# A two-layer convolution and a joint network on one core: weight sums in fp16, shift copies dropped, 378 direct outputs for 426

## The chip, the cores and the metric

The kernel runs on one core of a Trainium2 chip. The metric is device time in microseconds of one execution, given as the median of several runs. A separate execution was taken with the hardware profiler; its page and its trace are what the readings below come from. Engines are named as the profile names them: PE is TensorE's matmuls and PEld its weight loads, DVE is VectorE, ACT is ScalarE, POOL is GpSimd, SP is SyncE, which issues nearly all DMAs.

## What is computed

x is 2 x 4000 x 512 in bf16, w1 and w2 are five 512 x 512 taps each, and the three last weights are 512 x 512.

```python
xp = jnp.pad(x, ((0,0),(pad,pad),(0,0)))          # pad = 2
for i in range(5):
    h = h + einsum("btc,cd->btd", xp[:, i:i+T, :], w1[i])
h = gelu(h)[:, ::2, :]                             # 2 x 2000 x 512
# the same once more with w2:                        f = gelu(...)[:, ::2, :], 2 x 1000 x 512
fe = einsum("btd,de->bte", f, w_f)
ge = einsum("bud,de->bue", g, w_g)                 # g: 2 x 8 x 512
j = tanh(fe[:, :, None, :] + ge[:, None, :, :])    # 2 x 1000 x 8 x 512
return einsum("btud,dv->btuv", j, w_o)
```

## The kernel before

**Two ways to compute the first convolution.** A convolution with stride 2 and five taps needs 5 x 16 matmuls (four blocks of 128 input channels, four of output channels) per column of outputs. The kernel does the first `ND` = 426 outputs of the first sequence that way, tap by tap (`direct`, in the order `TAPS` = 0, 4, 2, 1, 3). All others are computed in triples (`Triple`, `Unit`): three neighbouring outputs come out of 9 products instead of 15, on sums and differences of x and on sums of the weight taps that are made once. A product of a triple is 16 matmuls over n columns for 3n outputs. The first sequence has a small set of `NF` = 190 triples (tile `xa`) and one of 336 (`xp1`); the second sequence has two of 334 (`xp2`, `xp0`). The second convolution is two more sets of 334 (`hT0`, `hT1`) on the first one's output. The tiles `row0` and `row1` hold the x differences of even samples, the planes of `xa` and `xp` are overwritten with those of odd samples.

**Getting x in.** For the direct part x is loaded in rows (`xr`): 512 rows with four samples a partition, then 384 rows with three a partition. `turn` transposes the first block on TensorE (16 transposes against `ident`), `turn3` the second with 12 matmuls against permutation matrices (`perm`) that POOL builds; ACT and DVE evict both to `eo`, split into even and odd samples. For the triples x comes through DMA transposes, six phases a set (samples 6q to 6q + 5).

**Weight sums.** `w1part` and `w2part` make the summed taps for one block of 128 output channels each: t = w0 + w4, v = t - w2, u = w0 + 4 w4 + 2 w2, t + w2, w1 - w3, w1 + w3, 2 w1. t, u and v are float32 (`ssum`, `wv`, `wu`, `ws`). u is made by two scalar_tensor_tensor on DVE (`stt`, line 655); ACT scales u and v by 1/3 into bf16, and makes 2 w1.

**x differences** (`step`, sums on line 494, copies on line 499). Three planes r = 2z - z' are made by an ACT copy with scale 2 and a DVE subtraction. Two more ACT copies, "next" and "prev", shift a plane by one column, so that the sums "ti" and "s0" read columns that start where their output starts.

**A unit** is one block of 128 output channels of one set. It runs its nine products into a PSUM bank of its own in five pieces; between these ACT copies the bank aside (tile `sd`) and DVE combines it (line 655, `acc<-acc,sd`), and ACT applies gelu. Units follow each other with one to two in flight.

**The joint part**, from about 130 us on, forms tanh on ACT and multiplies with w_o by a seven-product scheme on 2 x 2 blocks (`Seven`) whose operand sums go to POOL or DVE.

**Order.** Each engine's instructions are placed by a planner: every operation is recorded with what it reads and writes, and `schedule` lays them out with estimated costs; `once` is one pass, `learn` shifts priorities, and up to `PASSES` = 1200 passes are tried. Operations recorded with `flex` may go to ACT or DVE (or POOL or DVE); the planner picks. `emit` then adds the semaphore waits. All matmuls have one line in the profile, 507, all DVE sums line 494, all ACT operations line 499.

Of the kernel before, what the change touches and what calls it, by code (L numbers as in the profile page):

```python
# [12 lines left out]
P = 128  # L13
CELL = 4

# [53 lines left out]
class Plan:  # L69
# [4 lines left out]
    PASSES = 1200  # L74
# [85 lines left out]
    def schedule(self, pred):  # L160


        ops, HOP, n = self.ops, self.HOP, len(self.ops)
        succ = [[] for _ in ops]
        for i, p in enumerate(pred):
            for j in p:
                succ[j].append(i)
        span = [o.cost + (4.0 if o.dma else 0.0) for o in ops]
        late, nextpe = [0.0] * n, 0.0
        for i in range(n - 1, -1, -1):  # L170
            t = min([late[s] - (HOP if pred[s][i] else ops[i].cost - span[i]) for s in succ[i]], default=0.0)
            if ops[i].eng == "pe":
                t = min(t, nextpe)
            late[i] = t - span[i]
            if ops[i].eng == "pe":
                nextpe = late[i]
        hold = [0.0] * n
        best, tried = self.once(pred, succ, late, hold), 0
        for _ in range(self.PASSES):
            new = list(late), list(hold)  # L180
            if not self.learn(pred, best, *new, tried):
                break
            got = self.once(pred, succ, *new)
            if got[0] < best[0] + 1e-9:
                tried = tried + 1 if got[0] > best[0] - 1e-9 else 0
                best, (late, hold) = got, new
            else:
                tried += 1
        self.end, order, self.start, _, _, where = best
        for i, e in where.items():  # L190
            o = ops[i]
            o.eng, (o.fn, o.cost), o.alt = e, o.alt[e], None
        return order

    def learn(self, pred, got, late, hold, tried):


        _, order, start, end, ready, _ = got
        place = {i: (e, p) for e, o in order.items() for p, i in enumerate(o)}
        gaps, t = [], 0.0  # L200
        for i in order["pe"]:
            if start[i] - t > 0.05 and start[i] > 6.0:
                gaps.append(i)
            t = end[i]
        if not gaps:
            return False
        kind, which = divmod(tried, len(gaps) + 1)
        if kind >= 6:
            rng = np.random.default_rng([13, tried])
            t = start[gaps[int(rng.integers(len(gaps)))]]  # L210
            for e in ("act", "dve"):
                for j in order[e]:
                    if t - 10.0 < start[j] < t and rng.random() < 0.15:
                        late[j] += float(rng.normal())
            return True
        step, wait = ((0.1, True), (0.5, False), (0.0, True), (2.0, True), (0.3, False), (1.0, True))[kind % 6]
        first = list(late)
        for i in gaps if which == len(gaps) else gaps[which:which + 1]:
            j = i
            for _ in range(30):  # L220
                done = [(end[q] + (self.HOP if w else 0.0), q) for q, w in pred[j].items()]
                if not done:
                    break
                q = max(done)[1]
                if self.ops[q].dma:
                    break
                e, p = place[q]
                if e in ("act", "dve") and p and start[q] > ready[q] + 0.03:
                    b = order[e][p - 1]
                    if wait and start[b] < ready[q] - 0.02 and first[b] > first[q]:  # L230
                        hold[b] = max(hold[b], ready[q] - 0.01)
                    late[q] -= step
                j = q
        return True

    def once(self, pred, succ, late, hold):


        ops, HOP, n = self.ops, self.HOP, len(self.ops)
        left = [len(p) for p in pred]  # L240
        ready = list(hold)
        free = {e: 0.0 for e in ("pe", "act", "dve", "pool", "sp")}
        cand = {e: [] for e in free}
        engines = [o.alt or (o.eng,) for o in ops]
        for i in range(n):
            if not left[i]:
                for e in engines[i]:
                    cand[e].append(i)
        order, where = {e: [] for e in free}, {}
        wire, lock, owner, start, done = 0.0, 0.0, None, [0.0] * n, [0.0] * n  # L250
        for _ in range(n):
            best = None
            for e, c in cand.items():
                if c:
                    t = max(free[e], min(ready[i] for i in c))
                    if best is None or t < best[0]:
                        best = (t, e)
            t, e = best
            now = [i for i in cand[e] if ready[i] <= t + 0.02]
            i = min(now) if e in ("pe", "sp", "pool") else min(now, key=lambda i: (late[i], i))  # L260
            for f in engines[i]:
                cand[f].remove(i)
            order[e].append(i)
            o = ops[i]
            cost = o.cost
            if o.alt:
                where[i], cost = e, o.alt[e][1]
            start[i] = t
            free[e] = t + cost
            if o.port:  # L270
                if owner != e and lock > t - 0.2 and e == "dve":
                    free[e] = max(t, lock) + cost + 0.2
                elif owner != e and lock > t:
                    free[e] = lock + cost
                lock, owner = free[e], e
            done[i] = end = free[e]
            if o.dma:
                wire = max(wire, t + 1.8) + o.wire
                end = max(wire, t + 2.0) + o.slack
            for s in succ[i]:  # L280
                ready[s] = max(ready[s], end + HOP if pred[s][i] else free[e])
                left[s] -= 1
                if not left[s]:
                    for f in engines[s]:
                        cand[f].append(s)
        return max(free.values()), order, start, done, ready, where
# [82 lines left out]
def bass_standalone__seq2seq_rnn_t_joint__speech_kernel(  # L369
# [26 lines left out]
    ND, NF = 426, 190  # L396
    NL = 2 * NT3 - ND // 3 - NF
    assert ND % 6 == 0 and NF % 2 == 0 and NL % 2 == 0
    EW = 16 + 4 * P
# [10 lines left out]
    with ExitStack() as es:  # L410
# [28 lines left out]
        ssum = [at(f"ssum{i}", [NK, P], FP32) for i in range(2)]  # L439
        geT = at("geT", [NK * BU], FP32)  # L440
        gT = at("gT", [NK, BU], BF16)
        zero = at("zero", [NT], BF16)
        ident, perm = at("ident", [P], BF16), at("perm", [3 * P // 2], BF16)
# [4 lines left out]
        assert eo.end <= w2_sb.end and ND < 4 * P  # L448
        xa = Buf(nc, "xa", [7, NK, 224], BF16, xs[0].end - xs[0].bytes)
# [70 lines left out]
        for i in range(3):  # L520
            pm = perm[i * P // 2:(i + 1) * P // 2]
            pl.op("pool", lambda e, pm=pm, i=i: e.affine_select(
                out=pm.ap, in_=zero[0:P // 2].ap, compare_op=ALU.not_equal, fill=1.0, base=-(i % 2),
                pattern=[[-2, P // 2]], channel_multiplier=1), (zero[0:P // 2],), (pm,))
# [7 lines left out]
        NR = (4, 3)  # L532
# [76 lines left out]

        def turn(pp, cost):  # L610
# [21 lines left out]
        def turn3(cost):  # L632
            n, h, lo = NR[1], P // 2, 16 + 2 * P
            for k in range(NK):
                c0 = (4 + k) * NT
                at_k = ps.cols(c0, 2 * n * h)

                def fn(e, k=k, c0=c0):
                    for r in range(n):
                        if r % 2:  # L640
                            o, pm = ps.h[:, c0 + 2 * h:c0 + 4 * h], perm.h[:, h:3 * h]
                        else:
                            o = ps.h[:, c0:c0 + NT].rearrange("p (s c) -> p s c", c=h)[:, r // 2:r // 2 + 5:4, :]
                            pm = perm.h[:, 0:2 * h].rearrange("p (s c) -> p s c", s=2)
                        ins = e.matmul(o, lhsT=xr[1].h[:, r, k, :], rhs=pm, start=r == 0, stop=r == n - 1,  # L645
                                       skip_group_check=True)
                    return ins
                pl.op("pe", fn, (xr[1][0:n], perm[:]), (at_k,), cost / NK)
# [10 lines left out]
        def w2part(m, part):  # L659
            sl = slice(m * P, (m + 1) * P)  # L660
            w = lambda i: w2_sb[i, :, sl]
            t, v, u = ssum[0][:], ssum[1][:], ws[0][:]
            if part == "s":
                tt("dve", t, w(0), w(4), add)
                tt("dve", v, t, w(2), sub)
# [694 lines left out]
```

## Time and profile before

| | |
|---|---|
| Time, median of 3 runs | 251.72 us (251.39 to 251.92) |
| Profiled execution, span from first to last instruction | 249.7 us |
| Median time beyond that span | 2.0 us |
| PE busy, share of the span | 245.6 us, 98% |
| DVE busy | 209.2 us, 84% |
| ACT busy | 210.4 us, 84% |
| POOL busy | 99.3 us, 40% |
| Granted TensorE clock | 1.00 |

The profiled execution has no other time than its span; the 2.0 us are the median of the runs less this span. In the rows of the profile, `out<-in` are the program's tile names, then come shapes and types, a count, and for groups the busy time and the mean duration of one in ns. In a timeline the first number is the start and the second how long the row's instructions took together. What stands in brackets is how long the engine was idle before it, and what ended that. Durations of neighbouring DVE and ACT rows overlap somewhat, so the distance between starts is what one of them costs its engine.

### The profile page before, as it was taken

How to read it: one execution, taken by the hardware profiler on the slowest of the kernel's cores; microseconds unless marked ns; L12 is line 12 of the kernel's file. 1: busy time of each engine (PE TensorE's matmuls, PEld its weight loads, DVE VectorE, ACT ScalarE, POOL GpSimd, SP SyncE). 2: the span in 40 equal slices, each digit the busy share in tenths (PEclk: the TensorE clock that was granted, in tenths of full speed). 3: DMA queues.
4: the chain of work that ended last, by engine and by line, in shares of the span. 5: the costliest groups of instructions: out<-in, count | busy, mean ns of one | idle time of the engine just before them, and what ended most of it. 6: DMA issues, size and time to landing. Idle time of an engine off the chain costs nothing.

```text
span 249.7 us, 5278 instructions
## 1 busy us (share of the span) xinstructions
PE 245.6 (98%) x1948; PEld 183.4 (73%) x1948; DVE 209.2 (84%) x354; ACT 210.4 (84%) x350; POOL 99.3 (40%) x109
## 2 busy tenths in 40 slices
PE   8999999999999999999999999999999999999994
PEld 4977976666666666667556888777888878777883
DVE  1899998957999999398957879778999989986783
ACT  3499998869778668883599999999999999998772
POOL 2000000000000000000007978979799899888830
PEclk9999999999999999999999999999999999999999
DMA  7999999989000052000001043323345554455456
GB/s 236 327 209 198 159 209 133 183 188 340 4 3 0 0 179 77 0 4 0 0 3 42 14 149 110 109 86 124 101 161 167 171 189 158 160 182 181 147 193 207
DMA packets 54487, 31.86 MB, mean 128 GB/s; under 512 B 31518, under 2 KB 54206, under 8 KB 54462
## 3 DMA queue, kind: packets, MB, share of 16 engines
q1 hardware_dynamic: 54174, 31.37, 47.3%
q8 instruction: 15, 0.25, 0.4%
q10 hardware_dynamic: 288, 0.16, 0.2%
q14 instruction: 10, 0.08, 0.1%
HBM read 7.73 MB, written 16.38 MB: 97 GB/s over the span
## 4 chain that ended last, share of the span: by engine, by line
PE 98%; ACT 0%; ACTq 0%; issue 0%
PE acc L507 97%; PE acc L618 1%; PE acc L645 0%; ACT og L1067 0%; ACTq L1093 0%; ACT ost L499 0%; ACTq L330 0%
## 5 line engine op out<-in xcount | busy, mean ns | idle before, releaser
L494 DVE TENSOR_TENSOR og<-acc,sn 128x512 bf16<-128x512 f32 x84 | 54.9, 682 | 7.9 <-PE acc L507 7.5
L499 ACT ACTIVATE jT<-feT,geT 128x1000 bf16<-128x1000 f32 (+5 forms) x60 | 57.5, 1017 | 0.3 <-DVE feT L494 0.3
L1147 POOL TENSOR_TENSOR ss<-jT 128x512 f16<-128x512 bf16 x33 | 38.4, 1169 | 41.3 <-DVE ss L1147 40.9
L507 PE MATMUL acc<-tw,ss 128*128 128x256 f16 x336 | 46.2, 273 | 0.0
L507 PE MATMUL acc<-row,w_sb 128*128 128x334 bf16 (+2 forms) x224 | 38.8, 296 | 0.0
L507 PEld LDWEIGHTS acc<-tw,ss 128*128 128x128 f16 x336 | 32.3, 98 | 7.5 <-ACT sn L1067 0.5
L507 PE MATMUL acc<-wo_sb,jT 128*128 128x256 bf16 (+1 forms) x208 | 33.2, 285 | 0.0
L1067 ACT ACTIVATE sn<-acc 128x512 f32<-128x512 f32 x48 | 29.7, 628 | 3.2 <-PE acc L507 2.3
L1068 DVE COPY sn<-acc 128x512 f32<-128x512 f32 x36 | 24.6, 685 | 7.0 <-PE acc L507 6.7
L507 PEld LDWEIGHTS acc<-row,w_sb 128*128 128x128 bf16 x224 | 21.0, 97 | 9.3 <-DVE acc L655 1.0
L491 POOL MEMSET hT<- 128x8 bf16 (+2 forms) x6 | 0.8, 148 | 59.9 <-ACT hT L499 44.0
L507 PEld LDWEIGHTS acc<-wo_sb,jT 128*128 128x128 bf16 x208 | 20.3, 98 | 5.0
L499 ACT ACTIVATE sd<-acc 128x334 f32<-128x334 f32 (+2 forms) x48 | 20.5, 436 | 3.6 <-PE acc L507 3.0
L1147 POOL TENSOR_TENSOR ss<-ss,jT 128x512 f16<-128x512 f16 x19 | 21.9, 1156 | 0.8 <-DVE ss L1147 0.8
L499 ACT ACTIVATE hT<-acc 128x334 bf16<-128x334 f32 (+3 forms) x36 | 15.3, 439 | 6.8 <-PE acc L507 6.6
L655 DVE SCALAR_TENSOR_TENSOR acc<-acc,sd 128x334 f32<-128x334 f32 (+2 forms) x24 | 11.6, 483 | 9.3 <-PE acc L507 9.1
L494 DVE TENSOR_TENSOR row<-row 128x1336 bf16<-128x1336 bf16 (+2 forms) x24 | 18.9, 796 | 0.0
L499 ACT ACTIVATE jX<-feT,geT 128x1000 bf16<-128x1000 f32 (+3 forms) x20 | 18.4, 969 | 0.0
L507 PE MATMUL acc<-hT,w_t 128*128 128x334 bf16 x96 | 17.6, 304 | 0.0
L507 PE MATMUL acc<-xp,w_t 128*128 128x334 bf16 (+1 forms) x96 | 17.4, 305 | 0.0
L507 PE MATMUL acc<-wo_sb,ss 128*128 128x256 bf16 x112 | 17.3, 273 | 0.0
L507 PE MATMUL acc<-xp,w_x 128*128 128x334 bf16 (+1 forms) x96 | 16.8, 305 | 0.0
(127 smaller groups left out, 495.2 us busy)
## 6 DMA issues: line engine op xcount, KB each, us to landing
out_dram<-og SPq DMA_DIRECT2D x42, 256.0 KB, 2.2
w_sb<-in_w_dram SPq DMA_DIRECT2D x10, 512.0 KB, 5.4
out_dram<-og SPq DMA_DIRECT2D x14, 128.0 KB, 2.1
out_dram<-ost SPq DMA_DIRECT2D x10, 128.0 KB, 1.9
xr<-in_x_dram SPq DMA_DIRECT2D x1, 512.0 KB, 3.5
wf_sb<-in_w_f_dram SPq DMA_DIRECT2D x1, 512.0 KB, 3.6
wg_sb<-in_w_g_dram SPq DMA_DIRECT2D x1, 512.0 KB, 4.6
wo_sb<-in_w_o_dram SPq DMA_DIRECT2D x1, 512.0 KB, 5.8
```

The source lines that it names most:

```text
L491: pl.op("pool", lambda e: e.memset(v.ap, 0.0), (), (v,))
L494: pl.op(eng, lambda e: e.tensor_tensor(out=o.ap, in0=a.ap, in1=b.ap, op=op), (a, b), (o,), 0.02 + 2.14e-3 * o.ap.free_size() if eng == "po ...
L499: pl.op("act", lambda e: e.activation(o.ap, i.ap, func, scale=scale, bias=0.0 if bias is None else bias.ap), rd, (o,), o.ap.free_size() * ...
L507: ins = e.matmul(o.ap, lhsT=l.ap, rhs=r.ap, start=start and n == 0, stop=stop and n == len(pairs) - 1, skip_group_check=not check)
L618: ins = e.transpose(pv.ap[:, r, k - k0, :], xr[0].h[:, 2 * r + pp, k, :], ident.h[:, :])
L655: pl.op(eng, lambda e: e.scalar_tensor_tensor(out=o.ap, in0=a.ap, scalar=f, in1=b.ap, op0=ALU.mult, op1=add), (a, b), (o,), vec_cost(o, (a ...
L1067: pl.flex({"act": (lambda e: e.activation(o.ap, v.ap, ACT.Copy), 0.05 + n * 0.833e-3), "dve": (lambda e: e.tensor_copy(out=o.ap, in_=v.ap) ...
L1068: "dve": (lambda e: e.tensor_copy(out=o.ap, in_=v.ap), 0.065 + n * 1.04e-3)}, (v,), (o,))
L1147: fn = lambda e, o=S[i], x=x, y=y, op=op: e.tensor_tensor(out=o.ap, in0=x.ap, in1=y.ap, op=op)
```

## The change

- `ND` goes from 426 to 378 and `NF` from 190 to 206. The 336 triples after them stay. The 378 outputs need two samples a partition of the second row block, so 256 rows are loaded for 384, and `turn_more` makes 8 transposes (against `ident`) and two evictions where `turn3` made 12 matmuls and two evictions. `perm` and its three POOL instructions go. The direct part's matmuls on the second block go from 172 to 124 columns, its whole ones from 426 to 378, and the first set's triples from 190 to 206.
- t, u, v and the scaled copies of taps are fp16 or bf16 (`hw`, `hv`, on the bytes of the old float32 tiles). u is made of two scaled copies and two sums, all on 16-bit operands.
- A scaled copy (`scaled`) may go to ACT or to DVE. So may the factor-2 copies of x. In the order that is written out, DVE has the three of `xa` and ACT nearly all others of x; of the weight copies ACT has more.
- "next" and "prev" go; "ti" and "s0" read one column off.
- `schedule` has no passes any more: each engine's order is written out as a table (`ORDER`), 345 DVE rows, 308 ACT rows and so on, and it fixes where the `flex` operations go. The table also deals some of the joint part's matmuls and sums in another sequence.

```diff
-    ND, NF = 426, 190
+    ND = 378
+    NF = 332 - ND // 3
-        NR = (4, 3)
+        NR = (4, 2)
...
+        def turn_more(cost):
+            for pp in range(2):
+                bk, lo = 4 + pp, 16 + 2 * P
+                pv = View(psb[:, bk * 1024:bk * 1024 + NK * P], np.array([bk]), True)
+
+                def fn(e, pv=pv, pp=pp):
+                    for k in range(NK):
+                        ins = e.transpose(pv.ap[:, k * P:(k + 1) * P], xr[1].h[:, pp, k, :], ident.h[:, :])
                     return ins
+                pl.op("pe", fn, (xr[1][0:2], ident[:]), (pv,), cost / 2)
+                evict(None, eo[pp, :, lo:lo + P], pv.map(lambda a: a.rearrange("p (k c) -> p k c", k=NK)))
...
+        def scaled(o, v, f):
+            n = o.ap.free_size()
+            pl.flex({"act": (lambda e: e.activation(o.ap, v.ap, ACT.Copy, scale=f), 0.105 + n * 0.833e-3),
+                     "dve": (lambda e: e.tensor_scalar_mul(out=o.ap, in0=v.ap, scalar1=f), 0.065 + n * 0.26e-3)}, (v,), (o,))
...
         def w1part(m, part):
-            u, v, t = wu[m][:], ssum[m % 2][:], wv[m][:]
+            t, a, u, b, v = (hw[5 * m + i][:] for i in range(5))
+            a, b = (View(q.ap.bitcast(BF16), q.cells, False) for q in (a, b))
             if part == "04":
-                stt("dve", u, w(4), 4.0, w(0))
+                scaled(a, w(4), 4.0)
+                tt("dve", u, w(0), a, add)
                 tt("dve", t, w(0), w(4), add)
             else:
-                stt("dve", u, w(2), 2.0, u)
-                act(w1_x[1, :, sl], u, ACT.Copy, scale=1.0 / 3.0)
+                scaled(b, w(2), 2.0)
+                tt("dve", u, u, b, add)
+                scaled(w1_x[1, :, sl], u, 1.0 / 3.0)
                 tt("dve", v, t, w(2), sub)
-                act(w1_x[0, :, sl], v, ACT.Copy, scale=1.0 / 3.0)
+                scaled(w1_x[0, :, sl], v, 1.0 / 3.0)
...
-                elif which == "next":
-                    act(r(3), r(0, 1), ACT.Copy)
-                elif which == "prev":
-                    act(z(2), z(5, -1), ACT.Copy)
...
-                                     "tm": (r(5), r(2), r(1), sub), "ti": (r(3), r(1), r(3), sub),
+                                     "tm": (r(5), r(2), r(1), sub), "ti": (r(3), r(1), r(0, 1), sub),
-                                     "s0": (z(2), z(2), z(3), sub), "si": (z(5), z(5), z(1), sub),
+                                     "s0": (z(2), z(5, -1), z(3), sub), "si": (z(5), z(5), z(1), sub),
...
+        ops, order = self.ops, {}
+        for e, text in ORDER.items():
+            at, order[e] = 0, []
+            for word in text.split():
+                at += int(word)
+                order[e].append(at)
+                if ops[at].alt:
+                    ops[at].eng, (ops[at].fn, ops[at].cost), ops[at].alt = e, ops[at].alt[e], None
```

More of the change, by code (lines that the diff above doesn't have):

```diff
@@ L160, in schedule @@
     def schedule(self, pred):
[L163 to L189, printed above, removed]
@@ L190, in schedule @@
-        for i, e in where.items():
-            o = ops[i]
-            o.eng, (o.fn, o.cost), o.alt = e, o.alt[e], None
-        return order
[L195 to L286, printed above, removed]
@@ new lines, in schedule @@
+        ops, order = self.ops, {}
[6 more added lines that the diff above has]
+                    ops[at].eng, (ops[at].fn, ops[at].cost), ops[at].alt = e, ops[at].alt[e], None
+        assert sorted(i for o in order.values() for i in o) == list(range(len(ops)))
+        done, free, place = {}, dict.fromkeys(order, 0.0), dict.fromkeys(order, 0)
@@ new lines, in schedule @@
+        self.start, wire = {}, 0.0
+        while len(done) < len(ops):
+            before = len(done)
+            for e, o in order.items():
+                while place[e] < len(o) and all(j in done for j in pred[o[place[e]]]):
+                    i = o[place[e]]
+                    place[e] += 1
+                    t = max([free[e]] + [done[j] + self.HOP for j, w in pred[i].items() if w])
+                    self.start[i], free[e] = t, t + ops[i].cost
+                    done[i] = free[e]
+                    if ops[i].dma:
+                        wire = max(wire, t + 1.8) + ops[i].wire
+                        done[i] = max(wire, t + 2.0) + ops[i].slack
+            assert len(done) > before
@@ L439, in bass_standalone__seq2seq_rnn_t_joint__speech_kernel @@
         ssum = [at(f"ssum{i}", [NK, P], FP32) for i in range(2)]
+        hw = [Buf(nc, f"hw{i}", [NK, P], FP16, o) for i, o in enumerate(
+            v.end - v.bytes + q for v in wu + wv + ssum for q in (0, 1024))]
+        hv = [Buf(nc, f"hv{i}", [NK, P], FP16, o) for i, o in enumerate(
+            v.end - v.bytes + q for v in ssum + ws for q in (0, 1024))]
         geT = at("geT", [NK * BU], FP32)
@@ L442, in bass_standalone__seq2seq_rnn_t_joint__speech_kernel @@
         zero = at("zero", [NT], BF16)
-        ident, perm = at("ident", [P], BF16), at("perm", [3 * P // 2], BF16)
+        ident = at("ident", [P], BF16)
         warm = at("warm", [2], FP32)
@@ L447, in bass_standalone__seq2seq_rnn_t_joint__speech_kernel @@
         eo = Buf(nc, "eo", [2, NK, EW], BF16, w2_sb.end - w2_sb.bytes)
-        assert eo.end <= w2_sb.end and ND < 4 * P
-        xa = Buf(nc, "xa", [7, NK, 224], BF16, xs[0].end - xs[0].bytes)
+        assert eo.end <= w2_sb.end and ND < 3 * P
+        xa = Buf(nc, "xa", [7, NK, 16 * -(-(NF + 2) // 16) + 16], BF16, xs[0].end - xs[0].bytes)
         assert xa.end <= xs[0].end
@@ L608, in bass_standalone__seq2seq_rnn_t_joint__speech_kernel, with evict @@
         psb = ps.h[:, :].bitcast(BF16)
+        def evict(eng, o, v):
+            if eng is None:
+                n = o.ap.free_size()
+                pl.flex({"act": (lambda e: e.activation(o.ap, v.ap, ACT.Copy), 0.05 + n * 0.833e-3),
+                         "dve": (lambda e: e.tensor_copy(out=o.ap, in_=v.ap), 0.065 + n * 1.04e-3)}, (v,), (o,))
+            elif eng == "act":
+                act(o, v, ACT.Copy)
+            else:
+                pl.op("dve", lambda e: e.tensor_copy(out=o.ap, in_=v.ap), (v,), (o,), vec_cost(o, (v,)))
         def turn(pp, cost):
@@ L661, in w2part @@
             w = lambda i: w2_sb[i, :, sl]
-            t, v, u = ssum[0][:], ssum[1][:], ws[0][:]
+            t, a, u, b, v = (hv[(5 * m + i) % len(hv)][:] for i in range(5))
+            a, b = (View(q.ap.bitcast(BF16), q.cells, False) for q in (a, b))
             if part == "s":
@@ L673, in w2part @@
                 tt("dve", w2_t[3, :, sl], w(1), w(3), sub)
-                act(w(1), w(1), ACT.Copy, scale=2.0)
+                scaled(w(1), w(1), 2.0)
         def w1part(m, part):
@@ L690, in w1part @@
                 tt("dve", w1_t[1, :, sl], w(1), w(3), add)
-                act(w1_t[0, :, sl], w(1), ACT.Copy, scale=2.0)
+                scaled(w1_t[0, :, sl], w(1), 2.0)
         bank_a, bank_b = [4, 5, 6, 7], [0, 1, 2, 3]
@@ L1004, in bass_standalone__seq2seq_rnn_t_joint__speech_kernel @@
         units = [Unit(t, m) for t in trip for m in range(NK)]
-        STEPS = ("2d", "r", "t2", "t1", "prev", "s1", "tm", "si", "sm", "next", "t0", "s0", "ti")
+        STEPS = ("2d", "r", "t2", "t1", "s1", "tm", "s0", "si", "sm", "ti", "t0")
         fixed = {}
@@ L1012, in steps @@
             when(slot, *[lambda w=w: trip[i].step(w) for w in STEPS[lo:hi]])
-        for w in ("planes", "t2", "tm", "sm", "t1", "s1", "prev", "next", "t0", "s0", "ti", "si"):
+        for w in ("planes", "t2", "tm", "sm", "t1", "s1", "ti", "t0", "s0", "si"):
             trip[0].step(w)
@@ L1062, in take @@
             return free.pop(0)
-        def evict(eng, o, v):
-            if eng is None:
-                n = o.ap.free_size()
-                pl.flex({"act": (lambda e: e.activation(o.ap, v.ap, ACT.Copy), 0.05 + n * 0.833e-3),
-                         "dve": (lambda e: e.tensor_copy(out=o.ap, in_=v.ap), 0.065 + n * 1.04e-3)}, (v,), (o,))
-            elif eng == "act":
-                act(o, v, ACT.Copy)
-            else:
-                pl.op("dve", lambda e: e.tensor_copy(out=o.ap, in_=v.ap), (v,), (o,), vec_cost(o, (v,)))
         def store2(jt, src, key):
```

73 lines of the change are left out of this document (34 added, 39 removed), and 30 rows, old and new, of the table ORDER.

## The prediction

> **What bounds the kernel now.** I read the page first: busy shares, the slices and the chain that ended last. Then came the table of windows, cut where the kernel changes its work, and then the timeline of the first 35 us, which is where the edit lies.
>
> ```profile
> PE 245.6 (98%) x1948; PEld 183.4 (73%) x1948; DVE 209.2 (84%) x354; ACT 210.4 (84%) x350; POOL 99.3 (40%) x109
> PE acc L507 97%; PE acc L618 1%; PE acc L645 0%; ACT og L1067 0%; ACTq L1093 0%; ACT ost L499 0%; ACTq L330 0%
> ```
> ```profile
> 0.00:4.28 4.28, 3.51 (x8) 1.05 (x9) 0.27 (x1) 1.49 (x2) 1.59 (x15) 1.00 0.58 178
> 4.28:21.26 16.98, 16.93 (x158) 13.56 (x158) 14.56 (x27) 12.45 (x22) 0.35 (x3) 1.00 1.11 271
> 21.26:31.04 9.78, 9.78 (x118) 9.40 (x117) 9.63 (x23) 9.50 (x23) 0.12 (x1) 1.00 1.07 167
> 45.00:130.00 85.00, 85.00 (x598) 56.46 (x597) 73.74 (x120) 64.20 (x116) 0.60 (x3) 1.00 0.25 70
> 80.00:90.00 10.00, 10.00 (x72) 6.84 (x71) 10.00 (x18) 7.02 (x14) 0.00 (x0) 1.00 0.00 0
> 130.00:240.00 110.00, 110.00 (x911) 87.92 (x910) 93.31 (x160) 106.64 (x164) 96.16 (x85) 1.00 0.40 132
> ```
>
> The chain is TensorE from end to end. The windows (PE, weight load, DVE, ACT, POOL, clock, DMA share, GB/s) show it busy for all of each stretch from 4.28 us on but 0.05 us, at a clock of 1.00. Busy is not yet dense: matmuls overlap, so I count how many start. Between 80 and 90 us 72 start, almost all 334 columns wide: 10.00 / 72 = 139 ns, or 0.416 ns a column. TensorE streams, and a column less is time less, if its operands come as early as they are then needed. The stretch that could fail this is 4.28 to 31 us, where DVE is busy 14.56 of 16.98 us and then 9.63 of 9.78.
>
> **The columns.** Each matmul of the edit, by rows of the timeline (start, duration, engine, operation):
>
> ```profile
> 0.77 3.57 PE L507 MATMUL acc<-const-bfloat16-1.0 128*128 128x512 bf16 x8 [0.77 <-PEq L1345]
> 4.28 1.61 PE L618 MATMUL acc<-ident,xr 128*128 128x128 bf16 x16
> 9.44 0.83 PE L645 MATMUL acc<-perm,xr 128*128 128x128 bf16 x12
> 10.11 11.31 PE L507 MATMUL acc<-eo,w_sb 128*128 128x254 bf16 x96
> 21.26 1.15 PE L507 MATMUL acc<-xa,w_x 128*128 128x190 bf16 x12
> 22.25 0.49 PE L507 MATMUL acc<-row,w_x 128*128 128x190 bf16 x4
> 22.57 0.49 PE L507 MATMUL acc<-xa,w_x 128*128 128x190 bf16 x4
> ```
>
> The 12 permuting matmuls of 128 columns start 10.11 - 9.44 = 0.67 us before what follows, 56 ns each, which is 128 x 0.416 and 2.5 ns more. The 190-wide ones start four in 0.32 to 0.33 us (22.25 to 22.57), 82 ns. So I price a matmul at 0.416 ns a column and 2.5 ns. As a test on the direct part: 16 x 108 + 48 x 74 (172 columns) + 32 x 180 (426) = 11.0 us, and the rows have 21.26 - 10.11 = 11.15.
>
> - Direct part: 48 matmuls go from 172 to 124 columns, 74 to 54 ns. I allow the 56 ns of the 128-wide row as a floor and take 55: -0.91 us. 32 go from 426 to 378, 180 to 160 ns: -0.64.
> - Second samples: 12 permuting matmuls become 8 transposes. At 56 ns each that is -0.22. The 16 transposes at 4.28 took 1.61 / 16 = 101 ns, and 8 of those would be +0.14. I take -0.22, because those 16 stand right behind the eight opening matmuls, whose 3.57 / 8 = 446 ns for 512 columns is twice the time of the later pace, and the eight new ones stand at 9.44.
> - Triples: 9 products of 16 matmuls go from 190 to 206 columns: 144 x 6.7 ns = +0.96.
>
> Sum -0.81 us, between -0.86 and -0.40. All of it is on the path. The other 1,712 matmuls keep their shapes and their count, though the written-out order deals some of them in another sequence. The start (x lands, eight warm-up matmuls) and the tail (the same last 24 matmuls, evictions and stores) stay.
>
> One rule of the Trainium skill speaks against this: TensorE: Matmul & The Clock Gate, section Back-to-back issue gap, gives 81 ns a matmul at 128 columns in a sustained stream, weight loads counted. By it the 48 narrowed and 8 turning matmuls would cost more than they do here and the sum would be about +0.6 us (an estimate from that figure). The twelve at 9.44 us with 56 ns disagree, so it stays a rival.
>
> **The sooner start.** TensorE wants its first triple matmul at 21.26 - 0.91 - 0.64 - 0.22 = 19.49 us. What must be there by then?
>
> ```profile
> 7.36 0.69 DVE L655 SCALAR_TENSOR_TENSOR wu<-w_sb 128x512 f32<-128x512 bf16 x1 [1.74 <-DMA w_sb<-in_w_dram]
> 11.10 1.28 DVE L494 TENSOR_TENSOR ssum<-ws,w_sb 128x512 f32<-128x512 f32 x2
> 12.30 0.68 DVE L494 TENSOR_TENSOR w_t<-ws,w_sb 128x512 bf16<-128x512 f32 x1
> 18.13 0.41 DVE L494 TENSOR_TENSOR w_x<-w_sb 128x512 bf16<-128x512 bf16 x1
> 18.47 0.55 DVE L494 TENSOR_TENSOR xa<-xa 128x760 bf16<-128x760 bf16 x1
> 18.94 0.55 DVE L494 TENSOR_TENSOR row<-row 128x760 bf16<-128x760 bf16 x1
> 19.40 0.68 DVE L494 TENSOR_TENSOR ssum<-wv,w_sb 128x512 f32<-128x512 f32 x1
> ```
> ```profile
> L494 DVE TENSOR_TENSOR twf<-wf_sb,twf 128x512 f16<-128x512 bf16 x2 | 0.8, 415 | 0.0
> ```
>
> From start to start a sum of 512 elements with a 32-bit operand holds DVE 0.60 us (11.10 to 12.30, two), one with 16-bit operands 0.34 (18.13 to 18.47), 760 elements 0.47. Sums from bf16 into fp16, as the new ones are, took 415 ns like the bf16 one: 0.34 as well. The xa sum stands at an odd column and takes the 0.55 of the aligned row, so the shift copies can go without cost to the sums that then read one column off.
>
> No row shows the new scaled copy (one 16-bit tensor, a constant) on DVE. A two-tensor sum of the same size is a ceiling as long as the pace follows 16-bit operands: 0.34 for 512 elements, 0.51 for 832. Half its time per element over the same 0.07 us is the floor: 0.20 and 0.29. The stated far end is the pace of the 32-bit rows, 0.60 and 0.93. I take the floor: from 32-bit to 16-bit rows the time per element halved, so it follows the bytes moved, and one operand less is read. The Trainium skill (VectorE: DVE Perf Modes, section The perf-mode tier table) has such an operation at four elements a cycle, twice the two-tensor rate; its figures would give about the same floor.
>
> Now DVE's queue in the new order. It starts at 7.36 with the landing of the second weight tap, does six sums and one scaled copy (2.2 us), and waits for the eight transposes (9.44 + 0.45 + 0.2 of latency = 10.1) to evict one (0.6): 10.7. Then, up to the x difference that the first triple reads: 12 sums of 0.34, four of 0.50 on x, two scaled copies of 512 and three of 832. That is 10.7 + 4.1 + 2.0 + 0.4 + 0.9 = 18.1 us, 1.4 ahead of 19.49. The next product to need DVE is the x side of the fifth group, at 19.49 + 16 x 0.088 = 20.9; it needs three more sums on weights and three on x, 2.5 us: 20.6. So 0.3 us of cover there. Each 0.1 us that the five scaled copies cost more on average takes 0.5 off it.
>
> ACT loses two shift copies in each of six triples, and three planes of the first:
>
> ```profile
> L499 ACT ACTIVATE xp<-xp 128x1336 bf16<-128x1336 bf16 x2 | 2.6, 1322 | 0.0
> L499 ACT ACTIVATE xa<-xa 128x760 bf16<-128x760 bf16 x1 | 0.8, 829 | 0.0
> ```
>
> That is about 10 x 1.3 + 2 x 0.8 = 15 us of ACT, for five more weight copies, net, at 0.6 in this stage. None of it is on the path as such (ACT had 64.20 of 85.00 us in the stretch to 130): it frees the queue ahead of what TensorE waits for. The second set of sums (w2) gets 20 x 0.26 = 5 us shorter on DVE, less 1.2 for six scaled copies there, hidden likewise.
>
> DMA: the last weight tap. SP issues it behind three x loads, each now 208 rows for 192.
>
> ```profile
> 10.45 0.58 SPq L530 DMA_DIRECT2D w_sb<-in_w_dram  x1
> ```
> ```profile
> DMA to landing us min/median/max: 4.5/5.2/6.1
> ```
>
> The first row is its issue, the second the landing times of the five loads of w_sb up to 45 us. At the longest it lands at 16.55 us. The last tap's 16 matmuls began at about 21.26 - 16 x 0.180 = 18.4, and will begin at 19.49 - 16 x 0.160 = 16.9: cover falls from 1.8 to 0.4. Ahead of it 128 KB of second samples go and 48 KB of x rows come, -0.3 us at the window's 271 GB/s; three transposes 8% longer may delay its issue by some 0.1 us each. I price it at nothing, at worst +0.3.
>
> **Stalls that stand now.** Rows in which the weight load waited:
>
> ```profile
> 23.67 0.28 PEld L507 LDWEIGHTS acc<-row,w_t 128*128 128x128 bf16 x4 [0.18 <-ACT sd L499]
> 28.05 0.29 PEld L507 LDWEIGHTS acc<-row,w_t 128*128 128x128 bf16 x4 [0.16 <-issue]
> 65.39 0.40 PEld L507 LDWEIGHTS acc<-row,w_t 128*128 128x128 bf16 x4 [0.26 <-ACT sd L499]
> 79.68 0.40 PEld L507 LDWEIGHTS acc<-row,w_sb 128*128 128x128 bf16 x4 [0.29 <-DVE acc L655]
> 179.38 0.33 PEld L507 LDWEIGHTS acc<-tw,ss 128*128 128x128 f16 x4 [0.26 <-ACT sn L1067]
> 188.67 0.33 PEld L507 LDWEIGHTS acc<-tw,ss 128*128 128x128 f16 x4 [0.19 <-ACT sn L1067]
> ```
>
> The loader runs ahead, so I put about half of these 1.34 us on TensorE: 0.67. The first, third and fourth wait for ACT or DVE in stages whose queues get shorter: about 0.36 can go. The new order may open its own; from 130 us ACT has 106.64 of 110.00 us and the order there trades one ACT eviction for DVE and one sum from DVE to POOL, so nothing is gained. I take -0.2, between -0.67 and +0.3.
>
> Sum: -0.81 - 0.2 = -1.0 us. The profiled span is 249.7, the median of the three runs 251.72, so 2.0 us lie around it; I leave them. **250.7 us**, which is a span of 248.7.
>
> A weight load by itself:
>
> ```profile
> L507 PEld LDWEIGHTS acc<-eo,w_sb 128*128 128x128 bf16 x128 | 11.3, 97 | 3.2 <-ACT eo L499 0.2
> ```
>
> **Rivals.** A run of this kernel scatters by 251.39 to 251.92, so 0.2%, 0.5 us, is about what can be told from no change.
>
> - Scaled copies at the pace of the two-tensor sums: two more by 0.14 and three by 0.22 make DVE 0.93 later, less 0.3 of cover: TensorE waits 0.6 at the fifth group. 251.3 to 251.5, the same within 0.2%. For it: those are the nearest rows. Against it: they read twice the bytes.
> - The other side: scaled copies at the 32-bit pace. Two by 0.40 and three by 0.64 more: 2.7 us late, less cover 2.4 us on TensorE: 250.7 + 2.4 = 253.1, slower. It decides from the point where the five together cost 1.3 us more than I take (0.3 cover, 1.0 gain), and it shows as DVE-ended waits at 20 to 23 us. For it: all scalar rows in the profile (scalar_tensor_tensor) run at that pace; against: all of those touch 32 bits.
> - Narrow matmuls bound by their weight load: at its 97 ns 48 + 8 of them cost 56 x 42 ns = 2.4 us more, 253.1. The row at 9.44 speaks against it.
>
> - The written-out order deals the joint stage worse: ACT at 97% there has no room. Five more waits like that at 179 us (0.15 each on TensorE) and the late tap (0.3) give 251.7: no change.
>
> **How the numbers follow.** Forecast 0.71. Two-tensor pace 0.10, late order or tap 0.07 (half of that slower). 32-bit pace 0.06, narrow matmuls 0.02, and 0.04 for an order that stalls by over 1.5 us. So faster by over 0.2% (under 251.2) 0.72, same 0.14, slower 0.14. The low end takes the best of the columns (-0.86), all the stalls (-0.67) and 0.3 of scatter: 249.9. The high end takes in the two-tensor pace and the joint stage with 0.3 of scatter, 252.0; the 253.1 cases are left out.
>
> **What would show it.** Right: first xa matmul near 19.5 us, xa matmuls 88 ns apart, the 124-wide ones 54 to 56; scaled copies on DVE 0.20 apart from the next; no DVE- or DMA-ended idle time before the first five groups; the ACT wait ahead of the first t1 product gone. Wrong: the first xa matmul past 20.5, a wait for w_sb at 17 us, 124-wide matmuls at over 70 ns, or more than 1 us of ACT- or POOL-ended waits from 130 us on.

## The result, and the profile after

The changed kernel takes 252.07 us, the median of 22 runs (251.55 to 253.96). The kernel before takes 251.73 us on the same chip (22 runs, 251.39 to 252.1). The ratio is 1.0026, 95% interval 1.0015 to 1.0037: slower by 0.26%, where 250.7 us and faster was forecast. The profiled execution took 251.77 us, of which the span is 249.9 us.

The page of the changed kernel, its busy shares and its chain:

```profile
PE 243.4 (97%) x1938; PEld 182.9 (73%) x1944; DVE 207.8 (83%) x369; ACT 196.8 (79%) x338; POOL 100.6 (40%) x107
PE 88%; ACT 5%; DMA 2%; DVE 1%; issue 1%; ACTq 1%; SPq 0%; DVEq 0%
PE acc L459 88%; ACT jT L451 2%; DMA w_sb<-in_w_dram 2%; ACT og L560 1%; ACT sn L560 1%; ACT jX L451 1%; ACTq L1037 1%; DVE og L446 1%; DVE sn L561 0%; DVE og L561 0%; PE acc L596 0%; SPq L486 0%; ACT ost L451 0%; DVEq L277 0%; ACTq L277 0%
```

The chain is no longer TensorE's alone. ACT has 5% of it, and its queue of DMA issues (ACTq) 1%, which is about 2.5 us of 249.9. Most of ACT's 5% lies between 184 and 199 us, where the chain runs through evictions and tanh while TensorE is all but busy throughout (109.74 of 110.00 us below); the 1% of ACTq lies at the end. The stages themselves look as forecast. In the table of windows of the changed kernel (PE, weight load, DVE, ACT, POOL, clock, DMA share, GB/s), cut where its own first xa and xp products start:

```profile
4.28:19.54 15.26, 14.56 (x152) 11.84 (x153) 12.57 (x35) 12.37 (x23) 0.24 (x2) 1.00 1.08 265
19.54:30.94 11.40, 11.40 (x130) 11.24 (x128) 11.21 (x26) 9.38 (x22) 0.24 (x2) 1.00 1.10 181
45.00:130.00 85.00, 85.00 (x599) 56.56 (x598) 70.54 (x127) 54.78 (x106) 0.60 (x3) 1.00 0.28 70
130.00:240.00 110.00, 109.74 (x908) 88.08 (x912) 97.86 (x160) 105.98 (x164) 98.17 (x86) 1.00 0.41 135
```

ACT fell from 64.20 to 54.78 us of the 85 up to 130 us, DVE from 73.74 to 70.54, at an unchanged clock of 1.00. (Of PE's matmuls six have no record: x1938 for x1944 of PEld.) TensorE's part of the edit, from the timeline (start, duration, engine, operation):

```profile
6.05 3.66 PE L459 MATMUL acc<-eo,w_sb 128*128 128x254 bf16 x32 [0.64 <-DMA w_sb<-in_w_dram]
9.54 0.61 PE L596 MATMUL acc<-ident,xr 128*128 128x128 bf16 x8
9.99 9.71 PE L459 MATMUL acc<-eo,w_sb 128*128 128x254 bf16 x96
19.54 1.23 PE L459 MATMUL acc<-xa,w_x 128*128 128x206 bf16 x12
20.61 0.52 PE L459 MATMUL acc<-row,w_x 128*128 128x206 bf16 x4
20.96 0.52 PE L459 MATMUL acc<-xa,w_x 128*128 128x206 bf16 x4
```

The 0.64 us of idle time in the first row are nearly all of the 0.70 that TensorE lacks in the stretch from 4.28 us: it waits there for the first weight tap. In the kernel before the transposes ahead of it took up that time, and the same matmuls started at 5.94 us, 0.11 sooner. The first xa matmul starts at 19.54 us; 19.49 was forecast, and it was 21.26 before. TensorE's last matmul of the kernel starts at 245.16 us against 246.22: 1.06 us sooner, where 1.0 was forecast. So the time is lost after TensorE is done. The end of the timeline, first of the kernel before:

```profile
245.38 0.60 ACT L1067 ACTIVATE og<-acc 128x512 bf16<-128x512 f32 x1 [0.49 <-PE acc L507]
246.01 0.40 ACTq L1093 DMA_DIRECT2D out_dram<-og  x1
246.09 0.44 SPq L1093 DMA_DIRECT2D out_dram<-og  x1
246.51 0.28 ACT L499 ACTIVATE ost<-acc 128x128 bf16<-128x128 f32 x1 [0.53 <-PE acc L507]
246.82 0.34 ACTq L1093 DMA_DIRECT2D out_dram<-ost  x1
```

and then of the changed kernel:

```profile
244.32 0.60 ACT L560 ACTIVATE og<-acc 128x512 bf16<-128x512 f32 x1 [0.49 <-PE acc L459]
244.94 0.38 SPq L1037 DMA_DIRECT2D out_dram<-og  x1
244.95 2.44 ACTq L1037 DMA_DIRECT2D out_dram<-og  x1
247.50 0.28 ACT L451 ACTIVATE ost<-acc 128x128 bf16<-128x128 f32 x1 [2.58 <-DMA out_dram<-ost]
247.80 0.34 ACTq L1037 DMA_DIRECT2D out_dram<-ost  x1
```

The same five steps, with one difference: ACT's issue of the first half of the split store takes 2.44 us for 0.40. The last eviction stands behind it on the same engine, starts 1.0 us later than before instead of 1.1 sooner, and the last store leaves at 247.80 for 246.82. The profile puts the eviction's 2.58 us down to a transfer of ost. That is hardly the cause: the wait ends 0.1 us after the issue does, and in the kernel before no such wait stands there. By these rows it is the instruction ahead of it on ACT, and the experiments bear that out.

From TensorE's last matmul to the end it was 249.72 - 246.22 = 3.5 us and is now 249.95 - 245.16 = 4.8.

### The profile page after: what moved, and what is told of

The parts are those of the page before. It is cut to its first block, busy times and chain, and to the rows that moved or that the text cites. A ratio compares the mean times of both kernels' runs of the same rounds, so it can differ in the third digit from the quotient of the medians.

```text
span 249.9 us, 5265 instructions
## 1 busy us (share of the span) xinstructions
PE 243.4 (97%) x1938; PEld 182.9 (73%) x1944; DVE 207.8 (83%) x369; ACT 196.8 (79%) x338; POOL 100.6 (40%) x107
## 4 chain that ended last, share of the span: by engine, by line
PE 88%; ACT 5%; DMA 2%; DVE 1%; issue 1%; ACTq 1%; SPq 0%; DVEq 0%
PE acc L459 88%; ACT jT L451 2%; DMA w_sb<-in_w_dram 2%; ACT og L560 1%; ACT sn L560 1%; ACT jX L451 1%; ACTq L1037 1%; DVE og L446 1%; DVE sn L561 0%; DVE og L561 0%; PE acc L596 0%; SPq L486 0%; ACT ost L451 0%; DVEq L277 0%; ACTq L277 0%
## 5 line engine op out<-in xcount | busy, mean ns | idle before, releaser
L1091 POOL TENSOR_TENSOR ss<-jT 128x512 f16<-128x512 bf16 x34 | 39.4, 1176 | 35.2 <-DVE ss L1091 33.4
L560 ACT ACTIVATE sn<-acc 128x512 f32<-128x512 f32 x49 | 30.3, 626 | 3.0 <-PE acc L459 2.8
L561 DVE COPY sn<-acc 128x512 f32<-128x512 f32 x35 | 23.8, 683 | 4.5 <-PE acc L459 4.2
L1091 POOL TENSOR_TENSOR ss<-ss,jT 128x512 f16<-128x512 f16 x18 | 21.0, 1172 | 2.7 <-DVE ss L1091 2.3
L1091 POOL TENSOR_TENSOR ss<-jT,ss 128x512 f16<-128x512 bf16 x17 | 20.0, 1177 | 2.1 <-DVE ss L1091 2.1
```

The lines of the kernel that those rows point to most:

```text
L560: pl.flex({"act": (lambda e: e.activation(o.ap, v.ap, ACT.Copy), 0.05 + n * 0.833e-3), "dve": (lambda e: e.tensor_copy(out=o.ap, in_=v.ap) ...
L561: "dve": (lambda e: e.tensor_copy(out=o.ap, in_=v.ap), 0.065 + n * 1.04e-3)}, (v,), (o,))
L1091: fn = lambda e, o=S[i], x=x, y=y, op=op: e.tensor_tensor(out=o.ap, in0=x.ap, in1=y.ap, op=op)
```

## The experiments

**The theories.** The trace also holds the packets by which engines receive their own program: queue q14 in blocks of 8 KB, for ACT among others, and q8 in blocks of 16 KB, for TensorE. In the changed kernel an 8 KB packet runs from 245.87 to 246.18 us, in the midst of the long issue. In the kernel before the corresponding one came at 238.49, beside an eviction, and nothing shows. Packets of q14 came when ACT stood near numbers 68, 194 and 320 of its instructions (waits counted), some 128 apart; the long issue is number 448 of ACT's program. The kernel before has 20 instructions more ahead of it (shift copies and waits), so that its issue is number 468. (The order table lists 339 operations for ACT and 369 for VectorE, not the 308 and 345 given under "The change".)

- Theory A: an issue at which ACT calls for its next block is held up by that. The change shortened ACT's program by 20 instructions and so put the issue on the call.
- Theory B: the issues of ACT and SP, 0.01 us apart now and 0.08 before, hinder each other.
- Theory C: weights and x that land late at the head make the loss, and the long issue is by the way.

**The changed kernel again.**

> The changed kernel as it is. All theories: a span of 249.8 to 252, TensorE's last matmul starting near 245.2 us, and ACT's issue of the first half of the split store near 244.95 us lasting 2.4 us rather than 0.4, so that the last eviction starts near 247.5. Time about 252.0, 0.1% over the kernel before.

It measured 251.8 us (12 runs, 251.51 to 253.3), ratio to before 1.0009 (0.9997 to 1.0021): nearer to no change in this sample. The issue took 2.43 us, the block came from 245.74 to 246.05.

**Eight instructions more on ACT.** Each wait is on the first two transfers, which landed long before, and is one instruction more in ACT's program (462 in all for 454); p is the place in ACT's order.

```diff
+        loads = [o for o in ops if o.dma][:2]
...
+                if name == "act" and 240 <= p < 248:
+                    for q in loads:
+                        e.wait_ge(q.sem, q.val)
                 ins = o.fn(e)
```

> The changed kernel with eight waits more on ACT, on semaphores that were reached long ago, one ahead of each of eight operations near 165 us. They move every later ACT instruction eight places on in its program and change nothing else. Theory A (ACT's instructions arrive in blocks of 128 through a DMA queue, and the issue of the store stands where the next block is called, number 448 of its program): the issue falls back to 0.4 us, the last eviction starts at 245.5, span 248.0 to 248.7, time 250.1 to 250.7, faster than before by 0.4 to 0.6%. Theory B (the issues of ACT and SP, 0.01 us apart, hinder each other): the issue stays at 2.4 us and the time at 252.0. Theory C (late landings at the head make the loss): time at 252.0 as well, with the issue as it may be.

The end of the timeline of that kernel:

```profile
244.29 0.60 ACT L565 ACTIVATE og<-acc 128x512 bf16<-128x512 f32 x1 [0.49 <-PE acc L464]
244.92 0.38 ACTq L1042 DMA_DIRECT2D out_dram<-og  x1
245.40 0.28 ACT L456 ACTIVATE ost<-acc 128x128 bf16<-128x128 f32 x1 [0.51 <-PE acc L464]
245.70 0.35 ACTq L1042 DMA_DIRECT2D out_dram<-ost  x1
```

0.38 us for 2.44, span 248.5, and 250.42 us (5 runs, 250.18 to 250.53), ratio 0.9947 (0.9934 to 0.996). The block now comes at 241.00, beside evictions. Of the ten packets on q14 two came 4.9 us sooner, this one and that at 187.1, and the others within 0.6 us of where they were: those two are ACT's. ACT and SP still issue 0.01 us apart (244.92 and 244.91), so B falls; TensorE's last matmul starts at 245.13 as in the changed kernel, so C falls. Instructions that do nothing bring 1.4 us by the medians of the same session (251.8 to 250.42).

**The same loss in the kernel before.** The same edit with `72 <= p < 180`: 108 instructions more, which make the issue number 576, one block behind 448.

> The kernel before with 108 such waits more on ACT, one ahead of each of 108 operations between about 45 and 128 us, which bring its store issue from number 468 of ACT's program to 576, that is 448 and one block of 128. Theory A: the loss appears without the change: the issue lasts 2.0 to 2.5 us rather than 0.40, span 251.2 to 251.8, time 253 to 253.8, slower by 0.6 to 0.9%; the waits themselves cost nothing (ACT is busy 64 of 85 us there) or a few tenths. Theories B and C: issue 0.4 us, time 251.7 to 252.0.

```profile
246.18 2.59 ACTq L1098 DMA_DIRECT2D out_dram<-og  x1
248.87 0.28 ACT L504 ACTIVATE ost<-acc 128x128 bf16<-128x128 f32 x1 [2.72 <-DMA out_dram<-ost]
249.18 0.34 ACTq L1098 DMA_DIRECT2D out_dram<-ost  x1
```

253.35 us (6 runs), ratio 1.0067 (1.0054 to 1.008), with 2.59 us for the issue where at most 2.5 was expected. The loss needs nothing of the change but the count of instructions; TensorE's last matmul starts at 246.39, 0.17 us later than without the 108.

**Two instructions more.** `240 <= p < 242`.

> The changed kernel with two such waits on ACT instead of eight: the store's issue stands as number 450 of ACT's program, two behind the place of the call, and the last issue as 453. Theory A, if it is the place alone: the issue takes 0.4 us, time 250.4 as with eight waits. Theory A, if it is the time that the fetch takes: the call comes with the eviction ahead of the issue, 0.6 us sooner, so that the issue is held up for 1.3 to 1.9 us instead of 2.4, time 250.9 to 251.6.

```profile
244.55 0.60 ACT L565 ACTIVATE og<-acc 128x512 bf16<-128x512 f32 x1 [0.49 <-PE acc L464]
245.18 1.34 ACTq L1042 DMA_DIRECT2D out_dram<-og  x1
246.62 0.28 ACT L456 ACTIVATE ost<-acc 128x128 bf16<-128x128 f32 x1 [1.47 <-DMA out_dram<-ost]
```

250.94 us (8 runs, 250.34 to 251.7), ratio 0.9965 (0.995 to 0.9979). The call now falls on the eviction ahead of the issue, and the issue waits out the rest of it. So it is the time of the delivery that counts, not the place alone.

**The first half of the store issued by SP.** In stores(), `((2 * r, "sp"), (2 * r + 1, "sp"))`, the operation moved in the written-out order accordingly.

> The changed kernel with the first half of the split store issued by SP instead of ACT, ahead of the second half. Theory A: nothing of ACT's issue is left to be held up; SP issues twice 0.4 us in a row, the last eviction starts at 245.5, span 248.0 to 249.0, time 250.1 to 251.0. Theory B: the same, since the two issues no longer meet. Theory C: 252.0, unchanged.

```profile
246.77 0.28 ACT L451 ACTIVATE ost<-acc 128x128 bf16<-128x128 f32 x1 [0.50 <-PE acc L459]
247.08 1.67 ACTq L1037 DMA_DIRECT2D out_dram<-ost  x1
```

251.27 us (12 runs, 251.03 to 252.74), ratio 0.9991 (0.9978 to 1.0003): theory A had expected at most 251.0. With two instructions less on ACT (the issue and a wait), its other issue, that of the last store, went from number 451 to 449 and met the block in turn. The expectation had overlooked that. (This profiled execution, with a span of 250.5, also lost 1.2 us on TensorE at 216 to 219 us, behind VectorE sums of which one took 2.16 us; only this one shows it.)

The issues beside the block's packet, from the traces (us):

| kernel | number of the issue | issue | block's packet | issue ends behind the packet |
|---|---|---|---|---|
| changed | 448 | 244.95 to 247.39 | 245.87 to 246.18 | 1.21 |
| changed, again | 448 | 244.83 to 247.26 | 245.74 to 246.05 | 1.21 |
| two more | 450 | 245.18 to 246.52 | 244.95 to 245.33 | 1.19 |
| first half by SP (last store) | 449 | 247.08 to 248.75 | 247.23 to 247.54 | 1.21 |
| before, 108 more | 576 | 246.18 to 248.77 | 247.26 to 247.57 | 1.20 |
| eight more | 456 | 244.92 to 245.30 | 241.00 to 241.60 | - |
| before | 468 | 246.01 to 246.41 | 238.49 to 238.80 | - |

Whenever the packet is still to come, or has ended less than 1.2 us before the issue starts, the issue ends 1.2 us behind it. What passes in these 1.2 us no run shows.

The Trainium skill (Runtime: NRT & Kernel Launch, section Instruction fetch mechanics) says that an engine's program arrives in blocks over a DMA queue of the engine's own, and that crossing into the next block costs little that shows. The traces agree where the call falls on an eviction (eight more, and the kernel before), and not where it falls on an issue: 2.0 us there. It gives 16 KiB a block; TensorE's are that, ACT's here 8 KB, under a queue number that other engines' blocks carry too.

**24 more, and eight once more.**

> The changed kernel with 24 such waits. Theory A: the call for ACT's next block comes 24 instructions ahead of the store, near 234 us, on an eviction; issue 0.4 us, span 248.5, time 250.2 to 250.6, the same as with eight. If the eight waits had helped by their delay, or by the order in which stores meet, 24 would give another time than eight.

250.74 us (5 runs, 250.39 to 250.88), ratio 0.9953 (0.9941 to 0.9965); issue 0.38 us, span 248.6. The median is 0.14 above the 250.2 to 250.6 expected, on another chip than the first five runs with eight. Against the kernel before the gain is the same as with eight within the intervals, so nothing speaks for a delay or an order of stores.

> The changed kernel with eight waits once more, for the spread of its times: the changed kernel gave 251.5 to 254.0 in 22 runs, the kernel before 251.4 to 252.1. If the spread comes with the held-up issue, the times stay within 250.1 to 250.8; if it comes from the order dealt to the joint stage, single times up to 252.5 appear here too. Median 250.4 either way.

250.57 us (6 runs, 250.15 to 251.35), ratio 0.9952 (0.9938 to 0.9967). Neither half of the expectation came as stated: one time, 251.35, lies above 250.8, and none near 252.5. All 11 times with eight waits keep to 1.2 us, for 2.4 in the 22 of the changed kernel and 1.8 in the 12 of its second sample. That a part of the spread goes with the held-up issue is likely, and not shown; what makes the spread stays open.

**The columns alone.** In the kernel before, planner and all, `ND, NF = 378, 206`.

> The kernel before with one part of the change alone: 378 outputs of the first stage tap by tap and 206 triples, for 426 and 190; weight sums, shift copies, second samples and the planner stay. By the prediction's columns -0.91 - 0.64 + 0.96 = -0.6 us, time 251.0 to 251.1, if DVE and ACT deliver in time; their queues are the old, longer ones and triples start 1.5 us sooner, so that waits ended by DVE or ACT near 20 to 24 us could take up to 1.5 us, 252.5. ACT's store issue keeps number 468 there, so that theory A expects 0.4 us for it.

252.18 us (9 runs), ratio 1.0021 (1.0012 to 1.0031): slower, with 0.40 us for the issue. The waits of that kernel between 15 and 30 us (engine, line, what it waited for, us, times, longest), TensorE's and its weight load's:

```profile
PEld acc L507 <- ACT sd L499: 0.8, 1, 0.8
PEld acc L507 <- DMA w_sb<-in_w_dram: 0.7, 1, 0.7
PEld acc L507 <- DVE xa L494: 0.7, 1, 0.7
PE acc L507 <- ACT sd L499: 0.5, 1, 0.5
PE acc L507 <- DMA w_sb<-in_w_dram: 0.3, 1, 0.3
PE acc L507 <- DVE xa L494: 0.3, 1, 0.3
```

By the starts of its matmuls TensorE lost 0.44 us to DVE ahead of the first triple and 0.70 to ACT ahead of a t1 product, 1.1 us together, and 0.45 to the last tap. The profiled execution was the slowest of the nine (252.71 us, 0.94 above the kernel before). The median lies 0.41 above, where the columns alone would have put it 0.6 below: 1.0 us of waits. The changed kernel has none of these waits in that stretch. So what the change does besides the columns is worth about 1 us there, though none of it is on the path as such: it lets the narrower stage come early. Which part of it does so this run doesn't separate. The sums in fp16 and the dropped shift copies are the likely ones: VectorE works without a gap from 7.93 us to TensorE's first triple at 20.88, most of that time on sums with a 32-bit operand at 0.60 us each. But the written-out order differs too, and the wait for the last tap belongs to the loads of x ahead of it, which are larger there.

**Blocks for another engine.** Open was whether a block for one engine also holds up an issue by another. The eight on ACT and 100 on TensorE (`120 <= p < 220` of its order).

> The changed kernel with the eight waits on ACT and 100 more on TensorE, one ahead of each of 100 operations before 130 us, to see whether an issue is also held up by a block for another engine. TensorE's blocks (16 KB each) came at 143.4, 160, 176, 191, 205, 221 and 235 us in the run with eight waits; 100 instructions more, of some 256 in a block, bring each of them 5 to 6 us earlier. If such a block holds up SP's issue of a store, the long issues at 143.4 (2.0 us) and 176.4 us (1.8) fall to 0.4 and others appear where the moved blocks now meet an issue. If those two issues are long for a reason of their own (the stores' data, the queue), they stay where they are. Time 250.3 to 251.0: SP's issues have other work beside them, and 100 waits on TensorE cost up to 0.5 us.

The three stores from 143 us on, with eight on ACT alone and with 100 on TensorE besides:

```profile
143.05 2.74 SPq L1042 DMA_DIRECT2D out_dram<-og  x3
```
```profile
143.33 1.23 SPq L1042 DMA_DIRECT2D out_dram<-og  x3
```

The two long issues of SP fell to 0.46 and 0.33 us. Others took their place, where the moved blocks now came: 1.24 us at 153.56 (block from 153.43 to 154.39), 0.99 at 230.28 (229.96 to 230.89) and 1.80 at 242.80 (242.98 to 244.20). SP's queue at the end, with eight on ACT alone:

```profile
242.14 1.20 SPq L1042 DMA_DIRECT2D out_dram<-og  x3
245.62 0.33 SPq L1042 DMA_DIRECT2D out_dram<-ost  x1
```

and with 100 on TensorE besides:

```profile
242.41 2.61 SPq L1042 DMA_DIRECT2D out_dram<-og  x3
247.22 0.44 SPq L1042 DMA_DIRECT2D out_dram<-ost  x1
```

SP's last issue comes 1.6 us later, ACT's issues stay at 0.38 and 0.35, and the span is 249.9 for 248.5; the one time, 251.66 us, lies above the 250.3 to 251.0 expected. Blocks for TensorE hold up SP's issues, then. In the middle of the kernel that cost TensorE nothing that shows: its last matmul starts at 245.13 us with the two long issues and at 245.40 without. At the end nothing hides it. This is one run, and TensorE's 0.27 us are in its time.

**The version that beats both** is the change with eight instructions that do nothing: 250.42 and 250.57 us in two samples, 0.5% below the kernel before.

## Why the prediction was wrong, point by point

- **Columns** (-0.81): right. In the first stages matmuls start 55.4 ns apart at 124 columns, 161.2 at 378 and 88.8 at 206; 55, 160 and 88 were taken. The rule of the Trainium skill that was weighed there (TensorE: Matmul & The Clock Gate, section Back-to-back issue gap: 81 ns at 128 columns) does not hold in this stream, and the rival of weight loads at 97 ns falls with it. The eight transposes start 9.99 - 9.54 = 0.45 us ahead of what follows, 56 ns each, as taken.
- **Scaled copies** (the floor, 0.20 and 0.29 us): right, by the timeline of VectorE:

```profile
7.63 0.29 DVE L609 TENSOR_SCALAR hw<-w_sb 128x512 bf16<-128x512 bf16 x1
7.83 0.42 DVE L446 TENSOR_TENSOR hw<-w_sb 128x512 f16<-128x512 bf16 x1
12.67 0.37 DVE L609 TENSOR_SCALAR row<-xa 128x832 bf16<-128x832 bf16 x1
12.96 0.59 DVE L446 TENSOR_TENSOR row<-row,xa 128x832 bf16<-128x832 bf16 x1
```

  From start to start 0.20 us for 512 elements and 0.29 for 832. The x difference that the first triple reads starts at 17.11 us and what follows it at 17.61, where the prediction had it done at 18.1. The rivals at the pace of the two-tensor sums and of 32-bit rows did not come.
- **The last tap** (nothing, at worst +0.3): right here; it landed at 16.70 us, 0.3 ahead of need, and TensorE did not wait.
- **Stalls** (-0.2): about right. The waits ahead of t1 products at 23.67 and 28.05 us are gone, and so is the one at 65.39; that at 79.68 fell from 0.29 to 0.21 us, those at 178 and 187 stay (0.27 and 0.19 us). The list left out six waits of 0.20 to 0.32 us, at 44 us and from 119 to 132; five of them stay. From the first xa matmul to the last matmul TensorE took 0.66 us more, where the columns alone give +0.96: -0.3 for the stalls. With the sooner start of 1.72 us this made the 1.06 us.
- **The step that failed** is "The start ... and the tail (the same last 24 matmuls, evictions and stores) stay". The instructions at the tail were the same, their time was not: the term set at 0 is +1.3 us in the profiled execution (4.8 for 3.5 us), because ACT's issue of the split store met the delivery of ACT's next block and took 2.44 us for 0.40. By the medians of one session the held-up issue costs 1.4 us (251.8 against 250.42). Of the 2.06 us by which the issue is longer than with eight waits, the end shows 1.5 (248.49 to 249.95): with eight instructions more the end comes 2.8 us behind the last issue's start, in the changed kernel 2.1; why, no run shows. The 2.0 us around the span, which the prediction left as they were, did hold: 2.2 in the first sample, 2.0 in the second, 1.9 with eight waits.
- **The rivals**: none of them held this. The 0.14 for slower lay on other mechanisms (the chances listed there add to 0.155 for slower and 0.71 for faster, not 0.14 and 0.72), and the measured 252.07 lies just above the range's 252.0. The forecast of 250.7 is about what the change gives once ACT's issue is off the call (250.42 to 250.74 in three samples), but that is not the kernel that was predicted.

It could have been asked. In the profile of before SP's issues of stores take 0.39 us in the median of 97, yet one takes 1.92 (at 144.66 us) and one 1.54 (at 176.73), both beside a 16 KB block. That showed an issue to have a price that its own work doesn't explain, and the change took instructions out ahead of the two issues that have no cover, ACT's at the end.

## What to carry to other kernels

A store's issue near the end of a kernel has little to hide behind (1.5 of the 2.06 us showed here); if it is longer than its like, look at what the trace moves on the instruction queues at that moment, and count the instructions ahead of it on that engine. An edit that adds or drops instructions anywhere ahead of it on the engine moves that meeting, so a gain or loss of 1 to 2 us may have nothing to do with what the edit computes; a few waits that are long satisfied, put ahead of idle time, tell it apart in one run. And a part that is off the path by the profile can still be what a part on the path needs: the narrower stage alone, without the rest of the change, lost 0.2%.

## What the runs showed of the hardware that was not expected

An issue of a DMA on ACT ended 1.2 us (1.19 to 1.21 in five traces) behind the packet that brought ACT's next 8 KB of instructions, if it started before that; evictions that met the packet showed no delay (0.60 us at 241.03 with eight waits more, 0.60 at 234.96 with 24, 0.59 at 238.25 in the kernel before). Blocks of 16 KB for TensorE held up issues on SP, by up to 1.8 us (2.21 us at 143.49 in the changed kernel, for 0.39). Not every one: in the changed kernel the issue at 205.06 us took 0.39 with such a block under way from 204.97 to 206.31, and only the next, at 205.92, took 0.8; with 100 waits on TensorE one at 199.27 took 0.37 beside a block from 198.77 to 199.91. What decides between them stays open.
